# Softmax of chunked attention: exp and row sums by chunk on ScalarE instead of one exp between VectorE steps

## The chip, the cores and the metric

The kernel runs on one core of a Trainium2 chip. The metric is the device time of one execution in microseconds, the median of several runs. A core has five engines with a queue each: TensorE (matrix products, PE in the profile), VectorE (DVE), ScalarE (ACT), GpSimd (POOL) and SyncE (SP), which here only issues transfers. Each queue is worked off in order. TensorE's clock has two levels, 1.2 and 2.4 GHz; the profile shows the granted level as a share of the upper one.

## The reference

Attention within chunks of 64 positions (8 batches, 8 heads, 576 positions, head size 64), then two feed-forward layers over the 4608 tokens (512 wide, hidden 2048). The softmax adds 1e-9 to its row sums.

```python
scores = scale * np.matmul(q_c, k_c.transpose(0, 1, 2, 4, 3))
scores = scores - np.max(scores, axis=-1, keepdims=True)
attn = np.exp(scores)
attn = attn / (np.sum(attn, axis=-1, keepdims=True) + 1e-09)
out = np.matmul(attn, v_c)
# first layer:  h = x @ w_in;  g = s * relu(h)**2 + b;  y = g @ w_out
# second layer: h = y @ w_in;  g = h * sigmoid(1.702 * h);  out = g @ w_out
```

## The kernel before

The tokens are cut into 9 blocks of 512. For each block, attention works on four pairs of heads: a pair fills 128 partitions (two heads of 64) and 8 chunks of 64 keys, so a tile of scores is 128x512. Every product of the feed-forward layers is done as three products of split numbers (a high part that ScalarE makes by a copy, a low part that VectorE makes by a subtraction). The weights of the first layer arrive as raw words and are decoded by steps that alternate between VectorE, GpSimd and ScalarE before they can be used (`decode`, lines 118 to 133; the split follows in 148 and 149).

The first hidden products (`gemm_in`, line 507, tile h) have two PSUM banks to write to; ScalarE's relu (line 533 for the first two blocks, 519 after) empties one, then it is squared, split (lines 98 and 99) and used two steps later by `gemm_out` (line 577, tiles acc). Blocks 0 and 1 are done first, while weights are still being decoded; then attention of block j+1 runs beside the first layer of block j. From about 870 us on there is no attention any more, only the second layer, in a scheme with fewer products (lines 607 to 796), with the sums of weights that it needs made beforehand (lines 210 to 224).

The softmax stands in `Pair.steps`, lines 300 to 330. Scores are computed on TensorE into a bank (tile sc, line 307). VectorE takes the maximum of each row and chunk (line 315) and subtracts it (line 316), ScalarE takes the exp of the whole tile in one instruction with the scale in it (line 320), VectorE sums each chunk (line 322), adds 1e-9, takes the reciprocal and multiplies (lines 323 to 325). Then p is turned: by 8 transposes on VectorE (line 281) for the later blocks, and by TensorE and a copy (lines 361 and 365) for the early ones. The second product follows (tile xT, lines 291 or 378), and the result is split into xh and xl.

`EarlyPair` is the form for blocks 0 and 1: there, q and k are turned by TensorE (line 348) and copied out of PSUM by ScalarE (lines 353 and 356). The scores and the results xT take turns in two banks (`at_ps`).

The order of the work comes from a list of items with due times (`at`, `steps_at`): each step of a pair, of a weight's decode and of the products has a time in units of half a product group. A planner then simulates the program with its own durations and fixes the order on each queue; a few orders are forced by hand (`behind`, and all transfers that are due before the time 2 * NS, in the order of the list).

Of the kernel before, what the change touches and what calls it, by code (L numbers as in the profile page):

```python
# [10 lines left out]
AF = mybir.ActivationFunctionType  # L11
ALU = mybir.AluOpType
AX = mybir.AxisListType
# [3 lines left out]
P = 128  # L17
CH = 64
# [26 lines left out]
def chunk_attention_two_ffn(ctx, tc, q, k, v, w1_in, w1_out, s, b, w2_in, w2_out, out):  # L45
# [6 lines left out]
    nc = tc.nc  # L52
# [9 lines left out]
    scale = 1.0 / float(D) ** 0.5  # L62
# [33 lines left out]
    def split(hi, lo, src):  # L96

        nc.scalar.activation(out=hi, in_=src, func=AF.Copy)  # L98
        nc.vector.tensor_tensor(out=lo, in0=src, in1=hi.bitcast(F32), op=ALU.subtract)  # L99


    def tmp(name, dtype=F32):
        return tpool.tile([P, NB_MAX], dtype, tag="tmp", name=name)
# [135 lines left out]
    class Pair:  # L239


        def __init__(self, j, hp):
            self.j, self.hp = j, hp
            self.n = sizes[j]
            self.nch = self.n // CH
# [23 lines left out]
        def stage_qk(self):  # L269
            self.qt, self.kt = tmp("qt")[:, 0:self.n], tmp("kt")[:, 0:self.n]  # L270
            for t, src in ((self.qt, self.raw[0]), (self.kt, self.raw[1])):
                nc.vector.transpose(out=t.rearrange("p (u l) -> p u l", l=BK), in_=src)
            yield
            yield
# [21 lines left out]
        def split_x(self, ps):  # L296
            X[0, self.j, self.hp] = xh, xl = new_x()
            split(xh, xl, ps)

        def steps(self):  # L300

            yield from self.stage_qk()
            yield
            ps = at_ps.tile([P, self.nch, CH], F32, tag="at", name="sc")
            for c in range(self.nch):
                for r in heads:
                    nc.tensor.matmul(  # L307
                        out=ps[r, c, :], lhsT=self.qt[r, c * CH:(c + 1) * CH], rhs=self.kt[r, c * CH:(c + 1) * CH],
                        start=True, stop=True,
                    )  # L310
            yield
            mx = spool.tile([P, self.nch], F32, tag="mx", name="mx")
            sm = spool.tile([P, self.nch], F32, tag="sm", name="sm")
            p = tmp("p")[:, 0:self.n].rearrange("p (c t) -> p c t", t=CH)
            nc.vector.tensor_reduce(out=mx, in_=ps, axis=AX.X, op=ALU.max)
            nc.vector.tensor_tensor(
                out=p, in0=ps, in1=mx.unsqueeze(2).to_broadcast([P, self.nch, CH]), op=ALU.subtract
            )
            yield
            nc.scalar.activation(out=p, in_=p, func=AF.Exp, scale=scale)  # L320
            yield
            nc.vector.tensor_reduce(out=sm, in_=p, axis=AX.X, op=ALU.add)
            nc.vector.tensor_scalar(out=sm, in0=sm, scalar1=1e-9, scalar2=None, op0=ALU.add)
            nc.vector.reciprocal(out=sm, in_=sm)
            nc.vector.tensor_tensor(  # L325
                out=p, in0=p, in1=sm.unsqueeze(2).to_broadcast([P, self.nch, CH]), op=ALU.mult
            )
            yield
            turned = self.turn(p)
            yield  # L330
            ps = self.second(turned)
            yield
            self.split_x(ps)
            done[0, self.j] = done.get((0, self.j), 0) + 1

    class EarlyPair(Pair):


        def __init__(self, early, hp):
            super().__init__(early.j, hp)  # L340
# [2 lines left out]
        def stage_qk(self):  # L343
            ps = []
            for x in ("q", "k"):
                ps.append(acc_ps.tile([P, self.n], F32, tag=f"acc{2 * (self.hp % 2) + len(ps)}", name="qkT"))
                for i in range(self.n // P):
                    nc.tensor.transpose(
                        ps[-1][:, i * P:(i + 1) * P], self.early.raw[x, i][:, self.hp * P:(self.hp + 1) * P], ident
                    )  # L350
            yield
            self.qt = tmp("qt")[:, 0:self.n]
            nc.scalar.copy(out=self.qt, in_=ps[0])
            yield
            self.kt = tmp("kt")[:, 0:self.n]
            nc.scalar.copy(out=self.kt, in_=ps[1])
# [489 lines left out]
    def plan_first_weights():  # L846
        for n, (kind, i) in enumerate(order):
            st = {}
            if n < KF:
                t = FIRST - (7 - 2 * n if n < 2 else 2.5 - 1.5 * (n - 2))  # L850
                t_load = FIRST - 20 + 1.5 * n if n < STAGED else t - 5
            else:
                t = FIRST + (15 + 1.5 * i if i < KF // 2 else 24 + 3.5 * (i - KF // 2))
                t_load = t - 5

            def load(kind=kind, i=i, st=st):
                st["st"] = load_first(kind, i)

            def steps(kind=kind, i=i, st=st, n=n):

                old = len(nc.cur_bb.bb.instructions)
                for step, _ in enumerate(first_steps(kind, i, st["st"])):
                    if step == 0:
                        behind(old, DVE, ("lo", n - 2))
                        behind(old, ACT, ("relu", n - 4))
                    yield
                marks["lo", n] = latest(DVE)
            at(t_load, load)
            steps_at([(t + d, 1) for d in (0, 0.8, 1.6, 2.3)], steps, after_x=n >= EARLY)
# [71 lines left out]
```

## Time and profile before

| | |
|---|---|
| time, median of 3 runs | 1655.84 us (1654.95 to 1659.75) |
| the profiled execution | 1655.53 us |
| its span, first to last instruction | 1653.8 us |
| TensorE busy | 1601.2 us, 97% |
| VectorE busy | 1046.3 us, 63% |
| ScalarE busy | 786.0 us, 48% |
| GpSimd busy | 278.8 us, 17% |

The shares of busy time are means over stages with different limits. Products are pipelined, so their durations overlap. In a row of a group, the first number after the bar is its busy time in us, then the mean of one instruction in ns, then the idle time of its engine just ahead of it and what ended it. An instruction that starts before the one ahead of it has ended overlaps with it.

### The profile page before, as it was taken

To read this page: it belongs to the slowest core of one execution; us is meant where nothing else is said; L and a number is where in the kernel's file an instruction comes from. 1 tells how busy PE (TensorE), PEld (TensorE's weight loads), DVE (VectorE), ACT (ScalarE), POOL (GpSimd) and SP (SyncE) were. 2 spreads that over 40 slices of the span, in tenths; PEclk is the share of its full clock that TensorE was granted. 3 is DMA by queue.
4 is the path that set the end of the run, shared out by engine and by line. 5 is a ranking of instruction groups with operands and counts; after the bars stand their busy time and mean duration, and the time that the engine had idled before them with its cause. 6 is when DMAs were issued, how large, how long until landed. Compare 5 with 4: busy or idle time off the path is not lost.

```text
span 1653.8 us, 24616 instructions
## 1 busy us (share of the span) xinstructions
PE 1601.2 (97%) x8936; PEld 1311.6 (79%) x8936; DVE 1046.3 (63%) x1724; ACT 786.0 (48%) x1339; POOL 278.8 (17%) x310
## 2 busy tenths in 40 slices
PE   6879999999999999999999999999999999999998
PEld 4668877778888888888888888878887888788876
DVE  5887765745565565656635443579558946984685
ACT  3766533444544444454446532456345535553552
POOL 1344201223314223232322000010001000100000
PEclk8889999999999999999999999999999999999999
DMA  9435455656555555655456441676868686777764
GB/s 228 116 102 156 122 134 129 149 134 164 132 147 142 138 140 147 159 140 139 127 158 200 139 123 43 192 249 214 205 194 264 183 223 205 254 187 219 217 194 76
DMA packets 398345, 272.19 MB, mean 165 GB/s; under 512 B 255376, under 2 KB 345488, under 8 KB 398224
## 3 DMA queue, kind: packets, MB, share of 16 engines
q1 hardware_dynamic: 390800, 249.64, 55.8%
q0 software_dynamic: 5120, 16.78, 3.1%
q10 hardware_dynamic: 2304, 4.20, 0.7%
q8 instruction: 71, 1.16, 0.3%
q14 instruction: 50, 0.41, 0.1%
HBM read 209.72 MB, written 60.82 MB: 164 GB/s over the span
## 4 chain that ended last, share of the span: by engine, by line
PE 90%; DVE 4%; ACT 2%; DMA 1%; POOL 1%; SPq 1%; issue 1%; ACTq 0%; POOLq 0%
PE acc L577 25%; PE h L507 23%; PE x L682 11%; PE x L777 11%; PE d L682 5%; PE d L777 5%; PE b L777 3%; PE b L682 3%; PE sc L307 2%; PE xT L291 2%; POOL wm L130 0%; SPq L255 0%; DVE wi L126 0%; DVE p L325 0%; DVE wi L149 0%
## 5 line engine op out<-in xcount | busy, mean ns | idle before, releaser
L507 PE MATMUL h<-xh,wi 128*128 128x512 f32 x1280 | 402.0, 396 | 17.6 <-ACT r L519 6.1
L577 PE MATMUL acc<-gh,wo 128*128 128x512 f32 x1152 | 356.7, 393 | 2.3 <-ACT gh L98 2.3
L507 PEld LDWEIGHTS h<-xh,wi 128*128 128x128 f32 x1280 | 240.0, 190 | 70.7 <-ACT r L519 7.9
L577 PEld LDWEIGHTS acc<-gh,wo 128*128 128x128 f32 x1152 | 215.3, 189 | 48.4 <-ACT gh L98 2.5
L507 PE MATMUL h<-xl,wi 128*128 128x512 f32 x640 | 250.6, 393 | 0.0
L577 PE MATMUL acc<-gl,wo 128*128 128x512 f32 x576 | 223.1, 392 | 0.0
L99 DVE TENSOR_TENSOR gl<-r,gh 128x512 fp32r<-128x512 f32 x128 | 95.4, 746 | 144.6 <-ACT gh L98 144.2
L507 PEld LDWEIGHTS h<-xl,wi 128*128 128x128 f32 x640 | 121.5, 190 | 26.0
L519 ACT ACTIVATE r<-h 128x512 f32<-128x512 f32 x112 | 66.3, 592 | 147.5 <-PE h L507 141.6
L577 PEld LDWEIGHTS acc<-gl,wo 128*128 128x128 f32 x576 | 108.4, 189 | 23.4 <-DVE gl L99 0.6
L130 POOL TENSOR_TENSOR wm<-wm,wc 128x512 int32<-128x512 int32 x52 | 72.2, 1392 | 293.5 <-DVE wm L126 129.6
L754 ACT ACTIVATE op<-wo 128x512 fp32r<-128x512 f32 x128 | 79.5, 630 | 79.3 <-PE d L777 25.8
L704 DVE TENSOR_TENSOR wo<-wo,r 128x512 f32<-128x512 f32 x96 | 66.0, 691 | 63.0 <-ACT r L703 62.6
L777 PE MATMUL x<-op,wi 128*128 128x512 f32 x432 | 104.4, 389 | 0.0
L621 POOL DMA_DIRECT2D xr<-y x32 | 17.2, 539 | 507.1 <-ACT r L703 262.8
L682 PE MATMUL x<-xh,wi 128*128 128x512 f32 x320 | 99.6, 391 | 3.1 <-DVE wo L701 3.1
L281 DVE STREAM_TRANSPOSE pt<-p 32x256 f32<-32x256 f32 x224 | 97.7, 436 | 3.9
L703 ACT ACTIVATE r<-wo 128x512 f32<-128x512 f32 x96 | 60.8, 633 | 76.7 <-DVE wo L701 76.0
L777 PEld LDWEIGHTS x<-op,wi 128*128 128x128 f32 x432 | 81.1, 188 | 16.9
L755 DVE TENSOR_TENSOR op<-wo,op 128x512 fp32r<-128x512 f32 x128 | 85.2, 680 | 7.4 <-ACT op L754 6.0
L218 ACT ACTIVATE wst<-wst 128x896 fp32r<-128x896 f32 x32 | 30.5, 953 | 119.2 <-POOL wst L216 69.1
L98 ACT ACTIVATE gh<-r 128x512 fp32r<-128x512 f32 x128 | 80.5, 629 | 13.5 <-DVE r L523 11.0
(148 smaller groups left out, 2768.2 us busy)
## 6 DMA issues: line engine op xcount, KB each, us to landing
wi<-wo_sums SPq DMA_DIRECT2D x112, 512.0 KB, 4.3
wi<-wi_sums SPq DMA_DIRECT2D x96, 512.0 KB, 3.7
wst<-in_moe_w_out SPq DMA_DIRECT2D x32, 512.0 KB, 4.5
wi_sums<-wst SPq DMA_DIRECT2D x32, 448.0 KB, 3.6
wo_sums<-wst SPq DMA_DIRECT2D x32, 448.0 KB, 3.5
wst<-in_moe_w_in SPq DMA_DIRECT2D x24, 512.0 KB, 5.1
y<-ost SPq DMA_DIRECT2D x36, 256.0 KB, 3.7
xr<-y POOLq DMA_DIRECT2D x32, 256.0 KB, 6.2
```

The lines of the kernel that those rows point to most:

```text
L98: nc.scalar.activation(out=hi, in_=src, func=AF.Copy)
L99: nc.vector.tensor_tensor(out=lo, in0=src, in1=hi.bitcast(F32), op=ALU.subtract)
L130: nc.gpsimd.tensor_tensor(out=t, in0=t, in1=c.bitcast(I32), op=ALU.add)
L281: nc.vector.transpose(out=pt[r.start + ek * BK:r.start + (ek + 1) * BK, :, eq * BK:(eq + 1) * BK], in_=p[r.start + eq * BK:r.start + (eq + ...
L507: nc.tensor.matmul(out=ps, lhsT=w_[:, kk, :], rhs=x_, start=kk == 0 and a == 0, stop=kk == KD - 1 and a == 2,)
L519: nc.scalar.activation(out=r, in_=ps, func=AF.Relu)
L577: nc.tensor.matmul(out=acc[m], lhsT=l_, rhs=r_, start=i == 0 and a == 0, stop=i == KF - 1 and a == 2)
L682: nc.tensor.matmul(out=self.ps[key], lhsT=l_, rhs=r_, start=start and k == 0 and a == 0, stop=k == HK - 1 and a == 2, skip_group_check=not ...
L704: nc.vector.tensor_tensor(out=g, in0=h, in1=r, op=ALU.mult)
L754: nc.scalar.activation(out=hi, in_=src, func=AF.Copy)
L755: nc.vector.tensor_tensor(out=lo, in0=src, in1=hi.bitcast(F32), op=ALU.subtract)
L777: nc.tensor.matmul(out=self.ps[key], lhsT=l_, rhs=r_, start=start and i == 0 and a == 0, stop=i == HF - 1 and a == 2, skip_group_check=not ...
```

## The change

After the maximum, VectorE no longer subtracts. The maximum is negated and scaled in its small tile, and eight instructions on ScalarE, one for each chunk of 64 columns, read the scores from PSUM, multiply by the scale, add the negated maximum as a bias from that tile, take the exp and give the row's sum as a second output. VectorE's sum over the tile is gone. In the early blocks the copy of q multiplies by -scale, so the scores come out negated and scaled, their minimum is the bias as it is, and the exp takes them times -1.

```diff
+        def bias(self, mx, ps):
+
+            nc.vector.tensor_reduce(out=mx, in_=ps, axis=AX.X, op=ALU.max)
+            nc.vector.tensor_scalar(out=mx, in0=mx, scalar1=-scale, scalar2=None, op0=ALU.mult)
+            return scale
+
...
-            nc.vector.tensor_reduce(out=mx, in_=ps, axis=AX.X, op=ALU.max)
-            nc.vector.tensor_tensor(
-                out=p, in0=ps, in1=mx.unsqueeze(2).to_broadcast([P, self.nch, CH]), op=ALU.subtract
-            )
-            yield
-            nc.scalar.activation(out=p, in_=p, func=AF.Exp, scale=scale)
-            yield
-            nc.vector.tensor_reduce(out=sm, in_=p, axis=AX.X, op=ALU.add)
+            to_exp = self.bias(mx, ps)
+            yield
+            for c in range(self.nch):
+                nc.scalar.activation(
+                    out=p[:, c, :], in_=ps[:, c, :], func=AF.Exp, scale=to_exp, bias=mx[:, c:c + 1],
+                    accum_out=sm[:, c:c + 1],
+                )
+            yield
...
     class EarlyPair(Pair):
 
+        def bias(self, mx, ps):
+
+            nc.vector.tensor_reduce(out=mx, in_=ps, axis=AX.X, op=ALU.min)
+            return -1.0
...
-            nc.scalar.copy(out=self.qt, in_=ps[0])
+            nc.scalar.activation(out=self.qt, in_=ps[0], func=AF.Copy, scale=-scale)
```

## Rows read from the trace of the kernel before

**Rows 1.** The page: busy us, share and count; the granted clock in 40 slices.

```profile
PE 1601.2 (97%) x8936; PEld 1311.6 (79%) x8936; DVE 1046.3 (63%) x1724; ACT 786.0 (48%) x1339; POOL 278.8 (17%) x310
...
PEclk8889999999999999999999999999999999999999
```

**Rows 2.** Stretches: length, then busy us of PE, PEld, DVE, ACT, POOL; clock; DMA.

```profile
0.00:45.00 45.00, 27.94 (x326) 20.82 (x327) 25.92 (x51) 17.71 (x33) 4.54 (x9) 0.87 1.08 226
45.00:125.00 80.00, 67.05 (x498) 52.65 (x497) 66.25 (x106) 55.09 (x103) 30.58 (x22) 0.88 0.35 105
...
260.00:350.00 90.00, 83.53 (x574) 66.99 (x573) 52.64 (x92) 35.61 (x59) 24.30 (x28) 1.00 0.58 145
350.00:860.00 510.00, 510.00 (x3326) 420.98 (x3325) 289.52 (x520) 236.73 (x391) 156.99 (x182) 1.00 0.54 140
```

**Rows 3.** One line's instructions, the exp: ns min/median/max, first and last start.

```profile
L320 ACT ACTIVATE p<-p x36: 615/630/635, 14.0 to 811.9; 128x512 f32<-128x512 f32 x36
```

**Rows 4.** TensorE's waits, 0 to 130 us: total, times, longest.

```profile
PE h L507 <- ACT r L533: 5.8, 4, 2.8
...
PE h L507 <- DVE wi L149: 3.8, 1, 3.8
```

**Rows 5.** The chain of waits, first pair: start us, us, what.

```profile
13.32 0.70 DVE p L316
...
15.43 0.18 DVE sm L323
```

**Rows 6.** Groups by line and shape, ScalarE.

```profile
L592 ACT ACTIVATE ost<-acc,shift,sb 128x512 f32<-128x512 f32 x18 | 13.8, 770 | 2.0 <-PE acc L577 1.7
...
L98 ACT ACTIVATE xh<-xT 128x256 fp32r<-128x256 f32 x16 | 5.5, 382 | 5.9 <-PE xT L378 5.8
...
L596 ACT COPY ost<-acc 128x512 f32<-128x512 f32 x2 | 1.2, 588 | 6.0 <-PE acc L577 6.0
L188 ACT COPY shift<-bw 128x4 f32<-128x4 f32 x1 | 0.2, 162 | 1.7 <-PE bw L185 1.7
```

**Rows 7.** The chain of waits, early stretch: start us, us, what.

```profile
61.31 0.60 DVE p L316
...
106.99 0.70 DVE sm L322
...
112.94 5.70 PE acc L577 x12
...
136.12 2.72 PE acc L577 x12
```

**Rows 8.** ScalarE in order of time, 0 to 45 us: start, us, instruction [idle before].

```profile
10.41 0.59 ACT L353 COPY qt<-qkT 128x512 f32<-128x512 f32 x1
10.89 0.60 ACT L356 COPY kt<-qkT 128x512 f32<-128x512 f32 x1
...
24.61 0.69 ACT L122 ACTIVATE wi<-wo 128x512 int32<-128x512 uint32 x1 [1.19 <-DMA wo<-in_moe_w_in]
```

**Rows 9.** ScalarE in order of time, from 43 us: two of its gaps.

```profile
67.11 0.67 ACT L122 ACTIVATE wi<-wst 128x512 int32<-128x512 uint32 x1 [1.96 <-DVE wi L126]
...
90.64 0.67 ACT L131 ACTIVATE wc<-wst 128x512 f32<-128x512 f32 x1 [1.37 <-POOL wm L130]
```

**Rows 10.** The chain of waits, 255 to 350 us.

```profile
268.48 0.70 DVE mx L315
...
295.37 3.02 PE h L507 x12
```

**Rows 11.** A full stretch in order of time: ScalarE, VectorE, then TensorE.

```profile
414.80 0.58 ACT L519 ACTIVATE r<-h 128x512 f32<-128x512 f32 x1
...
412.01 3.60 DVE L281 STREAM_TRANSPOSE pt<-p 32x256 f32<-32x256 f32 x8
...
419.04 0.61 PE L507 MATMUL h<-xh,wi 128*128 128x512 f32 x2
...
421.85 1.15 PE L291 MATMUL xT<-pt,vs 64*64 64x64 f32 x32
```

## The prediction

> **What bounds the kernel now.** I read the page first: busy times and granted clock. TensorE is busy 1601.2 of 1653.8 us, VectorE 63%, ScalarE 48% [rows 1]. So only the 52.6 us in which TensorE stands still, and what the clock takes in the first slices, can move at all. Then the table of stretches: of those 52.6 us, 45.00 - 27.94 = 17.1 lie before 45 us, 80.00 - 67.05 = 13.0 from 45 to 125, 90.00 - 83.53 = 6.5 from 260 to 350, and none from 350 to 860 [rows 2]. The remaining 16 us or so come after 860, where there is no softmax any more: its 36 exps run from 14.0 to 811.9 us [rows 3]. The change therefore works on two places with idle TensorE time and on one long stretch without any. Third, the waits of TensorE in the first 130 us: the first hidden product waits 3.8 us for decoded weights, and later products wait 5.8 us for their bank, which ScalarE's relu has not emptied [rows 4]. In that part the bound is the two engines that decode the weights, VectorE (66.25 of 80 us busy) and ScalarE (55.09 of 80), with TensorE at an average clock of 0.88, so partly at 1.2 GHz [rows 2].
>
> **The change, part by part.** Per pair of heads (36 of them, 8 early ones before 125 us, 28 later) VectorE loses the subtraction and the sum over 128x512. Each costs 0.70 us in a free chain and 0.60 us in a packed queue [rows 5, 7], so 1.2 to 1.4 us per pair. The 28 later pairs gain one scaling of 128x8, whose like took 0.18 us [rows 5]; the early ones have it in their copy of q, which stays one instruction on ScalarE and which I cost at nothing: it already reads the bank and writes the same tile.
>
> ScalarE loses one exp of 0.63 us [rows 3] and gains eight of 128x64. No row shows an exp of that size or one with a second output. From a copy out of PSUM of 512 columns (588 ns) and one of 256 (382 ns) a column is 0.80 ns, so 64 columns take 382 - 192 x 0.80 = 228 ns. Scale and bias read from tiles made the 128x512 line take 770 instead of 588 ns, so one such operand is 91 ns [rows 6]. That is 0.32 us each; two copies back to back start 0.48 us apart though they take 0.59, an overlap of 0.11 [rows 8]. Lower bound 0.21 us a piece, if the sum comes out for nothing; upper bound 0.32 + 0.16 = 0.48, if reading out the sum is one more instruction as long as the 128x4 copy [rows 6] and nothing overlaps. I take the middle, 0.34: a burst of 2.7 us (1.7 to 3.8). ScalarE's queue thus gets 2.7 - 0.52 = 2.2 us longer per pair. In the free chain of the first pair, from the start of the subtraction (13.32) to the add that follows the sum (15.43), 2.1 us pass now [rows 5]; then 2.7, plus 0.2 in later pairs. So the softmax of one pair gets about 0.6 us later (early) or 0.8 us later (later pairs). VectorE waits for the exp already now, at the sum; it will wait at the add, and behind that stand decode steps and the low halves of products: this is in the sums below. The scores' bank is held some 2 us longer, at no cost, since the pair's second product takes the other bank of the two. No transfer is moved, and nothing on SyncE's or GpSimd's queue.
>
> On the price of the burst, the Trainium skill, ScalarE: Activation LUTs, section What ACT_TABLE_LOAD costs, speaks against the change: an activation has a fixed part of about 280 ns when its bias is a pointer, 0.833 ns per column on top, and neighbours overlap by some 93 ns. By that (an estimate from the page) eight pieces take 8 x 0.24 + 0.09 = 2.0 us, without the readout of the sums, on which it gives no price; the burst would be 0.7 us shorter than mine and the sum below 4 x 0.7 = 2.8 us lower. The trace agrees on the parts it shows (overlap 0.11 us, operand 91 ns, slope 0.80).
>
> *Before 45 us*, four early pairs: -0.7 us. The subtractions and sums leave VectorE while it begins to decode. But ScalarE waits 1.19 us at 24.61 for the weights themselves [rows 8], so the first hidden product can come only about one VectorE instruction earlier. If the burst is 3.8 us, each pair is 1.7 us later instead, and its weights' decode behind it: bounds -2.0 and +1.7.
>
> *45 to 125 us*, the other four early pairs: +2.0 us. The chain of waits holds seven of their eight subtractions and sums (0.60 to 0.70, together 4.4 us; first and last in [rows 7]). They go. Four bursts come, 4 x 2.2 = 8.8 us more on ScalarE, and queued behind each are decode steps of weights, which VectorE waits for, and relus, for whose banks TensorE waits. ScalarE's queue has gaps after the first and third of these pairs, 1.96 us at 67.11 and 1.37 at 90.64 [rows 9], so I let a quarter of each burst vanish: 6.6 - 4.4 = 2.2, rounded to 2.0 since the last pair's mend the wait it already has. Bounds: -4.4 (bursts all in gaps) and +8.8 (VectorE's relief worth nothing).
>
> *260 to 350 us*: +0.8 us. Here a later pair's softmax is in the chain: max at 268.48, then through the turned p, an output, the decode of the second weights and transfers to the product at 295.37 [rows 10]. That path gets 0.8 us longer. ScalarE's own path (outputs and relu right behind the exp) gets 2.7 + 0.2 - 0.72 - 0.52 = 1.7 us longer, but waits that follow take up the difference. Bounds 0 and +1.7.
>
> *125 to 260 and 350 to 860 us*: 0. TensorE is full, and what covers the bursts is the distance between relu and the use of its bank. In the tight case shown, the relu at 414.80 ends at 415.38 and the group of products that needs a free bank starts at 419.04: 3.7 us for a burst that adds 2.2. The turned p is there at 415.61 and used at 421.85: 6.2 us for 0.8 [rows 11]. If that cover were gone each pair would cost up to 2.2 us, 62 us for 28; I allow two such pairs, +4, in the range.
>
> Sum: -0.7 + 2.0 + 0.8 + 0 = +2.1 us. The profiled execution took 1655.53 us (span 1653.8), 0.3 under the median of 1655.84, so 1658 us as a median. What a measurement of this kernel can tell from no change is about 0.3%, 5 us: the forecast is "no difference".
>
> **Rivals.** (1) *VectorE was the bound*: the bursts fall into ScalarE's gaps, and the 4.4 us of chain and another 1 to 2 before 45 us are gained: -0.7 - 4.4 = -5.1, at best -6.4, so 1650 us. For it: VectorE is the busier one of the two from 45 to 125 us, 83% against 69% [rows 2], and the chain holds its instructions, not the exps. Against: ScalarE would then be at (55.09 + 8.8)/80 = 80%, no freer than VectorE is now. (2) *ScalarE's queue becomes the wait*, between 45 and 113 us: each burst of the second block's four pairs stands ahead of a decode step and a relu, and nothing of VectorE's relief is used: +8.8, with +1.7 at 268 and about 0.5 before 45, 1667 us. It decides once a piece costs 0.40 us or more, or when bursts meet relus for whose bank TensorE already waits 5.8 us [rows 4]; against it stand the gaps of [rows 9]. (3) *Another order*: each queue's order comes from a planner that simulates the program with its own durations, and 252 more ScalarE instructions and other lengths give it another plan, also far from the softmax. A wait for a bank reached 2.8 us here [rows 4], and after a gap the 12 products at 112.94 took 5.70 us, where 12 of the same line at 136.12 took 2.72 (3.0 us lost, at the lower of the clock's two levels, 1.2 GHz for 2.4) [rows 7]; one of each and a little more is +8, 1664 us. (4) *The sums are not had for less*: if reading one out takes longer than the 128x4 copy, the work has only moved to ScalarE and grown; that is rival 2 with a burst over 3.8 us, and its chance is in there.
>
> **How the numbers follow.** Forecast 0.50 (its own range 1651 to 1661), rival 1 0.20, rival 2 0.20, rival 3 0.10. Faster by over 0.3% is rival 1: 0.20. Slower by over 0.3% is rivals 2 and 3: 0.30. Within: 0.50. The range reaches from rival 1's best (1649) to rival 2 (1667); beyond lie perhaps 2 in 10, the mishaps in full stretches above all.
>
> **What would show it.** In the changed profile: L316 and the 128x512 sum gone, VectorE some 45 us less busy; eight exps of 128x64 about 0.32 us long, starting 0.34 apart; ScalarE about 75 us busier; TensorE's busy time as before and 350 to 860 us still full; the idle time from 45 to 125 us at about 15 instead of 13.0. Rival 1 shows as a first full stretch that begins 5 us earlier, rival 2 as more waiting for relu or for decoded weights right after each early burst, rival 3 as waits far from any burst. The prediction is wrong if TensorE has new idle time after 350 us, or if the idle time before 125 us moves by more than 5 us either way.

## The result, and the profile after

The changed kernel takes 1668.03 us (median of 4 runs, 1666.82 to 1669.23) against 1656.16 for the kernel before on the same chip: ratio 1.0067, 95% interval 1.0051 to 1.0083, some 12 us slower. The forecast was 1658.0 and "no difference"; the time lies 1 us above the upper end of its range.

First the page of after, with its span and the busy time of each engine, as in [rows 1]:

```profile
span 1665.8 us, 25132 instructions
...
PE 1600.2 (96%) x8936; PEld 1310.7 (79%) x8936; DVE 1009.8 (61%) x1680; ACT 850.2 (51%) x1879; POOL 280.1 (17%) x310
```

TensorE does the same work as before (1600.2 us for 1601.2). The 12 us are time in which it stands still. VectorE has 36.5 us less to do and ScalarE 64.2 more. The groups of ScalarE show that each exp of 64 columns is two instructions, the exp itself and the readout of its sum, which overlap:

```profile
L324 ACT ACTIVATE p<-sc,mx 128x64 f32<-128x64 f32 x288 | 86.3, 326 | 49.0 <-DVE mx L303 26.6 <-DVE mx L346 13.5 <-issue 6.8
...
L324 ACT ACTIVATION_READ_ACCUMULATOR p<-sc,mx 128x1 f32 x288 | 63.2, 219 | 0.0
```

The stretches of after, with the columns of [rows 2] and one more stretch, 125 to 260:

```profile
0.00:45.00 45.00, 25.66 (x300) 19.42 (x304) 19.63 (x38) 22.29 (x88) 5.08 (x9) 0.96 1.01 222
45.00:125.00 80.00, 59.58 (x507) 46.19 (x504) 59.70 (x96) 60.34 (x159) 26.93 (x19) 0.91 0.34 100
125.00:260.00 135.00, 134.74 (x775) 109.34 (x774) 91.65 (x147) 72.16 (x175) 37.76 (x26) 1.00 0.51 138
260.00:350.00 90.00, 85.08 (x576) 68.62 (x575) 48.82 (x90) 41.67 (x117) 20.58 (x24) 0.98 0.55 133
350.00:860.00 510.00, 505.62 (x3322) 416.25 (x3321) 268.11 (x494) 269.13 (x683) 153.74 (x180) 1.00 0.53 138
```

TensorE's idle time from 45 to 125 us is now 80.00 - 59.58 = 20.4 us (13.0 before), before 45 us it is 19.3 (17.1), and 350 to 860 us, full before, has 4.4. Since stretches of equal time don't hold equal work, I also use the *lag*: the start of the n-th product of 512 columns in one kernel less its start in before. In after it is +2.0 us at 45 us, +0.5 at 61, where the second block's first burst starts, +5.7 at 125, +6.2 at 330, +9.4 at 350, +11.9 at 860 and +12.1 at the end. So half of the loss falls before 125 us, where eight pairs are worked off, and half near the later 28.

What TensorE waits for in the first 130 us of after (in us: total, times, longest; before it was [rows 4]):

```profile
PE h L517 <- ACT r L543: 12.6, 5, 4.7
...
PE sc L313 <- ACT kt L366: 4.7, 2, 4.3
...
PE qkT L358 <- DVE xl L99: 3.0, 1, 3.0
```

Waits for relu have grown from 5.8 to 12.6 us. ScalarE's timeline shows why. Lines of readouts and of most exps are left out; the bracket is the idle time ahead of an instruction:

```profile
13.42 0.31 ACT L324 ACTIVATE p<-sc,mx 128x64 f32<-128x64 f32 x1 [2.79 <-DVE mx L346]
...
15.75 0.64 ACT L363 ACTIVATE qt<-qkT 128x512 f32<-128x512 f32 x1
16.22 0.63 ACT L366 COPY kt<-qkT 128x512 f32<-128x512 f32 x1
...
75.53 0.64 ACT L98 ACTIVATE xh<-xT 128x256 fp32r<-128x256 f32 x2
78.40 0.31 ACT L324 ACTIVATE p<-sc,mx 128x64 f32<-128x64 f32 x1 [2.23 <-DVE mx L346]
...
80.63 0.24 ACT L324 ACTIVATION_READ_ACCUMULATOR p<-sc,mx 128x1 f32 x1
80.72 0.64 ACT L543 ACTIVATE r<-h 128x512 f32<-128x512 f32 x1
```

And TensorE's timeline beside it:

```profile
16.91 1.33 PE L313 MATMUL sc<-kt,qt 64*64 64x64 f32 x20 [4.26 <-ACT kt L366]
...
72.57 0.69 PE L388 MATMUL xT<-pt,wo 64*64 64x64 f32 x32
73.09 1.11 PE L313 MATMUL sc<-kt,qt 64*64 64x64 f32 x32
74.13 0.65 PE L358 MATMUL qkT<-ident,wo 128*128 128x128 f32 x4
77.82 0.66 PE L358 MATMUL qkT<-ident,wo 128*128 128x128 f32 x4 [3.03 <-DVE xl L99]
81.41 1.22 PE L517 MATMUL h<-xh,wi 128*128 128x512 f32 x2 [2.93 <-ACT r L543]
```

A burst lasts from 13.42 to 15.75, 2.33 us. The second pair's copies of q and k stand behind the first burst, at 15.75 and 16.22; in before they ran at 10.41 and 10.89, ahead of the exp [rows 8]. By 72.6 us both banks of the hidden products were full, so the rows show nothing that the relu at 80.72 waited for but its place in the queue. ScalarE stood still for 2.2 us, waiting for the maximum, then did the burst, then the relu. TensorE did two groups of transposes (qkT) in that time and waited 3.03 and 2.93 us. In before, hidden products stood between these two groups:

```profile
72.27 1.11 PE L348 MATMUL qkT<-ident,wo 128*128 128x128 f32 x4
73.03 1.20 PE L507 MATMUL h<-xh,wi 128*128 128x512 f32 x2
...
76.52 0.60 PE L348 MATMUL qkT<-ident,wo 128*128 128x128 f32 x4
```

The clock adds to the gap. TensorE was busy for 0.66 of the 4.4 us from 74.8 to 79.2, and from 79.2 to 86.0 us the granted clock was 0.50, which is 1.2 of 2.4 GHz: the twelve hidden products from 81.41 on took 5.2 us, the twelve from 86.75 on 3.0. Before has such a stretch too, but half as long (71.0 to 74.4).

The later half, on ScalarE around 345 us and on TensorE:

```profile
344.73 0.95 ACT L218 ACTIVATE wst<-wst 128x896 fp32r<-128x896 f32 x1 [9.66 <-POOL wst L216]
345.58 0.58 ACT L529 ACTIVATE r<-h 128x512 f32<-128x512 f32 x1
```

```profile
346.21 0.73 PE L517 MATMUL h<-xh,wi 128*128 128x512 f32 x2 [1.79 <-ACT r L529]
...
355.61 1.20 PE L517 MATMUL h<-xh,wi 128*128 128x512 f32 x2 [2.57 <-ACT r L529]
...
427.88 0.50 PE L587 MATMUL acc<-gl,wo 128*128 128x512 f32 x1 [1.49 <-DVE gl L99]
```

There a relu stands behind a step of the weight sums, which waits for GpSimd; the burst before it had ended ten us earlier, at 334.9. But the same stands in before:

```profile
338.25 0.95 ACT L218 ACTIVATE wst<-wst 128x896 fp32r<-128x896 f32 x1 [10.77 <-POOL wst L216]
339.11 0.58 ACT L519 ACTIVATE r<-h 128x512 f32<-128x512 f32 x1
```

From 125 to 860 us TensorE waits 7.5 us for relus in after and 6.1 in before, so these rows alone don't explain the later half. Two small things come on top: 2.1 us of waits for VectorE that before doesn't have, and a clock of 0.96 from 260 to 300 and 0.89 from 345 to 360 us, where before has 1.00.

### The profile page after: what moved, and what is told of

Its sections match the earlier page's. It is cut to its first block, busy times and chain, and to the rows that moved or that the text cites. A ratio compares the mean times of both kernels' runs of the same rounds, so it can differ in the third digit from the quotient of the medians.

```text
span 1665.8 us, 25132 instructions
## 1 busy us (share of the span) xinstructions
PE 1600.2 (96%) x8936; PEld 1310.7 (79%) x8936; DVE 1009.8 (61%) x1680; ACT 850.2 (51%) x1879; POOL 280.1 (17%) x310
## 4 chain that ended last, share of the span: by engine, by line
PE 83%; DVE 5%; SPq 3%; ACT 3%; DMA 3%; POOL 1%; issue 1%; ACTq 0%; POOLq 0%; DVEq 0%
PE h L517 22%; PE acc L587 21%; PE x L692 11%; PE x L787 11%; PE d L692 5%; PE d L787 5%; PE b L692 3%; PE b L787 3%; SPq L255 2%; PE sc L313 2%; PE xT L291 1%; ACT p L324 1%; POOL wm L130 1%; SPq L265 1%; DVE wi L149 1%
## 5 line engine op out<-in xcount | busy, mean ns | idle before, releaser
L517 PE MATMUL h<-xh,wi 128*128 128x512 f32 x1280 | 404.3, 398 | 25.4 <-ACT r L543 12.6
L99 DVE TENSOR_TENSOR gl<-r,gh 128x512 fp32r<-128x512 f32 x128 | 102.2, 799 | 138.8 <-ACT gh L98 138.2
L324 ACT ACTIVATE p<-sc,mx 128x64 f32<-128x64 f32 x288 | 86.3, 326 | 49.0 <-DVE mx L303 26.6
```

The source lines that it names most:

```text
L324: nc.scalar.activation(out=p[:, c, :], in_=ps[:, c, :], func=AF.Exp, scale=to_exp, bias=mx[:, c:c + 1], accum_out=sm[:, c:c + 1],)
L517: nc.tensor.matmul(out=ps, lhsT=w_[:, kk, :], rhs=x_, start=kk == 0 and a == 0, stop=kk == KD - 1 and a == 2,)
```

## The experiments

Each time is a median of 5 to 11 runs, and each ratio is to before on the same chip (1656.6 to 1656.8 us there), with its 95% interval. The theories: **the burst** (rival 2: ScalarE's queue is longer, so everything behind it is later), **the order** (rival 3: the planner puts the queues in another order), and one that came from the traces, **the claim**. Tile p is one of the shared pool `tmp` of ten buffers, from which relu's tiles (r), the turned q and k and decode's tiles come too. On a queue, the first writers of these tiles stand in the order in which the program asks for them. The traces bear that out for ScalarE up to 130 us: the copies of q and k and the relus come in one and the same order in before, after and all other kernels. In before p's first writer is VectorE's subtraction. In after it is the first exp, so a relu whose tile is asked for after p must stand behind that exp on ScalarE, even while the exp waits for the maximum.

### Which pairs

```diff
-            to_exp = self.bias(mx, ps)
+            if isinstance(self, EarlyPair):   # later_only: if not isinstance(...)
+                ...                           # the new softmax
+            else:
+                ...                           # the old one (later_only: q copied without a factor)
```

**early_only.** 

> The new softmax in the eight early pairs alone; the 28 later pairs keep subtraction, one exp and sum. In the trace of after, the products are 5.7 us late from 125 us on, and another 6.3 us come after 330 us. Bursts (rival 2): the 5.7 us come back here and nothing else, about 1661.8 us. Order of the planner alone (rival 3): no sum, any time from 1652 to 1668, and new waits far from any burst. VectorE's relief worth something in the later pairs: then this kernel must be slower than after minus 6.3, and the time would lie above 1662.

**later_only.** 

> The new softmax in the 28 later pairs alone; the eight early ones as before. Bursts: the idle time before 125 us is that of before (17 and 13 us), TensorE's waits at about 345, 427 and 674 us come back with 6.3 us, about 1662.5 us. If those waits hang on where the early part left the transfers and weight sums (the product stream 5.7 us late meets the sums of weights elsewhere), they don't come back: 1656 to 1658. Order of the planner alone: anything from 1652 to 1668.

Measured: early_only 1664.65, 1.0048 (1.0034 to 1.0062); later_only 1661.27, 1.0026 (1.0018 to 1.0035). The two losses, 0.48% and 0.26%, together make 0.74%, the 0.67% of after within their intervals: the halves are separate, and each comes without the other. The early pairs cost 3 us more alone than expected. In early_only the same waits stand as in after (12.6 us for relu, 4.3 for kt), and the lag is +6.2 at 125 us.

### The claim taken away

```diff
-            p = tmp("p")[:, 0:self.n].rearrange("p (c t) -> p c t", t=CH)
+            p = self.qt.rearrange("p (c t) -> p c t", t=CH)
```

**new_p_in_q.** 

> After, but p lives in the tile of qt, which is dead once the scores are made, and claims no buffer of the shared pool. The bursts have the same length and place of need. Theory of the claimed buffer: in after the first writer of p is an exp, so every relu, copy or decode step on ScalarE whose tile is handed out later than p's has to stand behind the burst, which waits for the maximum; with that gone ScalarE can take ready relus ahead of the burst, and most of the 12 us go: 1656 to 1660. Theory of the burst's length (rival 2): the queue is as long as in after, 1666 to 1669. Order alone: another number without a reason, 1654 to 1668.

**old_p_in_q.** 

> Before, with p in the tile of qt: the control for the kernel with the new softmax and p there. Claimed buffer: p's first writer is VectorE's subtraction, nothing on ScalarE waits for the claim, so 1655 to 1657. If the tenth buffer that comes free is worth something by itself, this kernel gains as well, 1650 to 1654. Order alone: up to 5 us either way.

Measured: new_p_in_q 1654.54, 0.9989 (0.9980 to 0.9998); old_p_in_q 1652.15, 0.9974 (0.9963 to 0.9984). With bursts as they were, the loss is gone; the time lies below the 1656 to 1660 that the claim foretold, as the buffer that comes free has a worth of its own. A buffer more is worth 4 us to the old kernel, and between these two kernels the change costs 0.15%, 2.4 us, where with p in the pool it costs 12.

To tell the claim from the buffer that comes free, VectorE touches p first, and, the other way round, the old exp claims it:

```diff
             p = tmp("p")[:, 0:self.n].rearrange("p (c t) -> p c t", t=CH)
+            nc.vector.memset(p[:, 0, 0:1], 0.0)        # new_touch: after
             to_exp = self.bias(mx, ps)
...
-                out=p, in0=ps, in1=mx.unsqueeze(2).to_broadcast([P, self.nch, CH]), op=ALU.subtract
+                out=d, in0=ps, in1=mx.unsqueeze(2).to_broadcast([P, self.nch, CH]), op=ALU.subtract
-            nc.scalar.activation(out=p, in_=p, func=AF.Exp, scale=scale)
+            nc.scalar.activation(out=p, in_=d, func=AF.Exp, scale=scale)   # old_exp_claims; d is qt's tile
```

**new_touch.** 

> After, with one tiny instruction more per pair: VectorE sets one column of p to zero ahead of the maximum (the exp overwrites it). Bursts, sizes and number of buffers are as in after, but the first writer of p's buffer is VectorE again, as in before. Theory of the claimed buffer: 36 instructions of about 0.1 us are paid on VectorE and most of the 12 us go, 1656 to 1661. If instead the gain of the kernel with p in the tile of qt came from the buffer that is left free, this stays at 1666 to 1669. Burst: 1666 to 1669.

**old_exp_claims.** 

> Before, with one edit: the subtraction writes into the dead tile of qt, and the one exp reads that and writes p. The instructions, their sizes and their number are those of before; only the first writer of p's buffer in the shared pool is now an exp on ScalarE, as in after. Theory of the claimed buffer: relus, copies and decode steps whose tiles are handed out after p's must stand behind the exp on ScalarE, so most of the loss comes without any burst: 1661 to 1668. Theory of the burst: nothing is longer, 1655 to 1657. Order alone: up to 5 us either way.

Measured: new_touch 1658.43, 1.0013 (1.0004 to 1.0022); old_exp_claims 1654.29, 0.9988 (0.9979 to 0.9997). The first went as the claim has it: 36 more instructions on VectorE and the kernel is 9.6 us faster than after. ScalarE, in new_touch:

```profile
68.67 1.10 ACT L544 ACTIVATE r<-h 128x512 f32<-128x512 f32 x2
...
73.72 0.31 ACT L325 ACTIVATE p<-sc,mx 128x64 f32<-128x64 f32 x1 [0.73 <-DVE mx L347]
```

The relus stand ahead of the burst, and the burst comes at 73.72 instead of 78.40. But the second refutes the claim by itself: there the relus do stand behind the exp, and it costs nothing. TensorE's waits for relus aren't a price by themselves either: before 130 us they are 9.2 us here, between the 5.8 of before and the 12.6 of after. ScalarE, in old_exp_claims:

```profile
70.82 0.61 ACT L321 ACTIVATE p<-qt 128x512 f32<-128x512 f32 x1
71.34 0.58 ACT L534 ACTIVATE r<-h 128x512 f32<-128x512 f32 x1
```

So neither a burst without the claim nor a claim without the burst makes the loss.

### Instructions and order exchanged

Every queue can be held to the order of another kernel (with p in qt's tile, so that no claim stands against it). The exps stand where the one exp stood; the subtraction goes right behind the maximum, the sum right ahead of the add:

```diff
+    for one, two in zip(row, row[1:]):      # row: all instructions, in the other kernel's order
+        tc.add_manual_dep(two, one.name, IN_ORDER, reason="fixed order")
```

**old_in_new_order.** 

> The old softmax (subtraction, one exp, sum; p in the tile of qt) with every queue held to the order of after: the exp stands where the burst's last exp stood, the subtraction right behind the maximum, the sum right ahead of the add. Order alone (rival 3): the order carries the loss, 1664 to 1668. Burst alone (rival 2 as it was forecast): without bursts nothing is lost, 1655 to 1658. Both together (the order puts relus and copies behind the exp, but only a burst of 2.3 us makes that dear): one exp of 0.6 us in that place costs little, 1657 to 1661.

**new_in_old_order.** 

> The new softmax (bursts with row sums; p in the tile of qt) with every queue held to the order of before: the eight exps stand where the one exp stood, the scaling where the subtraction stood. Relus that stood ahead of the exp still do. Order alone: 1655 to 1658. Burst alone: 1664 to 1668. Both together: the burst costs what was forecast for it, about 2 us, 1657 to 1660.

Measured: old_in_new_order 1664.84, 1.0046 (1.0033 to 1.0059); new_in_old_order 1657.86, 1.0010 (1.0001 to 1.0019). The order of after, with not one burst in it, carries 8 of the 12 us. The bursts, in the order of before, cost 1 to 2. TensorE in old_in_new_order has the two groups of transposes side by side as in after, and the waits around them:

```profile
68.87 1.22 PE L507 MATMUL h<-xh,wi 128*128 128x512 f32 x2 [2.61 <-ACT r L533]
...
74.84 0.66 PE L348 MATMUL qkT<-ident,wo 128*128 128x128 f32 x4
77.05 0.66 PE L348 MATMUL qkT<-ident,wo 128*128 128x128 f32 x4 [1.56 <-DVE xl L99]
79.58 1.22 PE L507 MATMUL h<-xh,wi 128*128 128x512 f32 x2 [1.87 <-ACT r L533]
```

I had thought that the claim hurts because each burst holds up a relu as it runs. That would have left old_in_new_order at 1657 to 1661, and it fell. Most of the loss is made when the order is planned. No kernel was held to its own order as a control; that holding is cheap is seen from new_in_old_order.

The same exchange between the two kernels with p in qt's tile:

**new_in_old_q_order.** 

> The new softmax, p in the tile of qt, with every queue held to the order of the old softmax with p there (1652.2). Burst priced by itself, as between before and the new softmax in its order (1.3 us): 1653 to 1656. If the burst's price was hidden there by chance: 1657 to 1661.

**old_in_new_q_order.** 

> The old softmax, p in the tile of qt, with every queue held to the order of the new softmax with p there (1654.5). If that order is a good one and the burst costs 1 to 2 us: 1652 to 1655. If the order holds a loss that the burst's relief on VectorE pays back: 1656 or more.

Measured: 1658.38, 1.0006 (0.9998 to 1.0015), and 1655.69, 0.9991 (0.9983 to 1.0000). By the ratios, the bursts cost 0.32% (5 us) in the order planned for the old softmax, and nothing (0.9989 with them, 0.9991 without) in the order planned for the new one. The first expectation was missed in its main range, and the second time lies between its two ranges. A burst's price isn't one number: it costs nothing that can be told in an order planned with it, and 1.7 and 5 us in two orders planned without it.

### Chance, or a plan that comes of itself?

Small edits that leave the softmax alone or nearly so:

```diff
+            nc.vector.tensor_scalar(out=sm, in0=mx, scalar1=-scale, scalar2=None, op0=ALU.mult)  # tiny_more: before; new_tiny: after
...
-            nc.scalar.activation(out=self.qt, in_=ps[0], func=AF.Copy, scale=-scale)   # new_plain_early: after,
+            nc.scalar.copy(out=self.qt, in_=ps[0])                                     # and no EarlyPair.bias
```

**tiny_more.** 

> Before, with one tiny instruction of 128x8 more on VectorE per pair, behind the maximum, whose result is overwritten: how far the planner's order and the time move without a cause of weight. Order alone (rival 3): several us, 1651 to 1664. Other theories: 36 times 0.06 us on VectorE, at most 0.5 us of it before 125 us, so 1656 to 1657.

**new_tiny.** 

> After, with one tiny instruction of 128x8 more on VectorE per pair behind the maximum, whose result is overwritten. Claim and burst are as in after; the planner gets another number of instructions. If the claim with the burst makes the slow order: 1664 to 1670. If the order is chance: anywhere from 1652 to 1668, most likely about 1658.

**new_plain_early.** 

> After, but the early pairs form their bias as the later ones do (maximum, then one scaling of 128x8 on VectorE, 0.1 to 0.2 us in the chain of each), and q is copied without a factor. Claim and burst as in after. If the claim with the burst makes the slow order: 1664 to 1671. If the order is chance: 1652 to 1668, most likely about 1658.

Measured: tiny_more 1656.84, 1.0000 (0.9991 to 1.0009); new_tiny 1670.86, 1.0071 (1.0057 to 1.0085); new_plain_early 1668.40, 1.0071 (1.0059 to 1.0084). Chance falls: one more instruction moves nothing in before, and three kernels with claim and burst, whose orders differ in places, have about the same loss.

### How long a burst

```diff
                     out=p[:, c, :], in_=ps[:, c, :], func=AF.Exp, scale=to_exp, bias=mx[:, c:c + 1],
-                    accum_out=sm[:, c:c + 1],
                 )
...
+            nc.vector.tensor_reduce(out=sm, in_=p, axis=AX.X, op=ALU.add)      # no_readout: both
...
-            for c in range(self.nch):                                         # no_readout_long: this as well
+            for c in [*range(self.nch), 0, 1, 2]:
...
+            nc.vector.tensor_reduce(out=sm, in_=p, axis=AX.X, op=ALU.add)      # readout_and_sum: after, and this alone
```

**no_readout.** 

> Eight exps by chunk with bias, but no second output: VectorE sums the tile as before. p in its own tile of the shared pool, claimed by the first exp. The burst has eight pieces some 0.2 us apart in place of 0.29, 1.6 to 1.9 us, and VectorE keeps a sum of 0.6 us per pair. Claim and burst together: the relus still stand behind a burst, 0.5 to 0.7 us shorter, 1662 to 1668. If reading out the sums is what costs: 1656 to 1659. Order alone: any of these.

**no_readout_long.** 

> The kernel without second outputs (1654.7), with three of its eight exps issued a second time, which write the same values again: the burst is 11 pieces of 0.21 us, about 2.4 us, as long as that of after; VectorE keeps its sum; p is claimed by the first exp. If the claim with a burst of over 2 us makes the slow order: 1663 to 1670. If it is the second output, or VectorE's missing sum: 1655 to 1659.

**readout_and_sum.** 

> After, with VectorE's sum over the tile kept beside the second outputs (it writes the same sums over them): 36 times 0.60 to 0.70 us more on VectorE. If the claim with the long burst makes the slow order: 1666 to 1673. If it is VectorE's missing sum, which lets the planner put other work there: 1655 to 1660.

Measured: no_readout 1654.69, 0.9988 (0.9979 to 0.9997); no_readout_long 1664.39, 1.0045 (1.0033 to 1.0058); readout_and_sum 1669.40, 1.0082 (1.0068 to 1.0096). ScalarE, in no_readout, then in no_readout_long:

```profile
72.33 1.71 ACT L324 ACTIVATE p<-sc,mx 128x64 f32<-128x64 f32 x8
73.90 0.63 ACT L543 ACTIVATE r<-h 128x512 f32<-128x512 f32 x1
```

```profile
78.42 1.71 ACT L324 ACTIVATE p<-sc,mx 128x64 f32<-128x64 f32 x8
79.99 0.63 ACT L543 ACTIVATE r<-h 128x512 f32<-128x512 f32 x1
80.47 0.77 ACT L324 ACTIVATE p<-sc,mx 128x64 f32<-128x64 f32 x3
```

Eight exps without readout take 1.57 us to the next instruction (72.33 to 73.90), 0.20 a piece, and with that the claim costs nothing: the expectation of 1662 or more was missed. Three more exps per pair, which compute nothing new, cost 9.7 us, and this pair's softmax comes 6 us later, as in after. Neither the readout as such nor VectorE's missing sum parts the kernels with the loss from the others. With the claim, exps of 0.6 to 1.6 us per pair are free here, 2.2 to 2.3 us are not. But the length doesn't work by holding up a relu as the burst runs: in the rows of no_readout_long the relu goes ahead of the three extra exps, behind 1.57 us as in no_readout.

What parts the kernels with the loss from those without it in the traces is where the planner put the maximum. Up to that of the last early pair, the copies of q and k, the relus and the first exps stand in the same order on ScalarE in all ten kernels in which the early exps claim p or are held to after's order, with the loss or without it (with it: after, new_tiny, new_plain_early, readout_and_sum, early_only, no_readout_long, old_in_new_order; without it: no_readout, one_exp, old_exp_claims). VectorE's order is not the same. Here it is in after, then in no_readout: the copy of the turned p, the decode step of line 133, and the maximum that the next burst waits for:

```profile
70.03 0.68 DVE L375 COPY pt<-pT 128x512 f32<-128x512 f32 x1
...
74.27 0.69 DVE L133 SCALAR_TENSOR_TENSOR wi<-wi 128x512 f32<-128x512 f32 x1 [0.20 <-ACT wi L131]
...
77.68 0.68 DVE L346 TENSOR_REDUCE mx<-sc 128x8 f32<-128x512 f32 x1
```

```profile
67.74 0.68 DVE L375 COPY pt<-pT 128x512 f32<-128x512 f32 x1
...
71.43 0.68 DVE L346 TENSOR_REDUCE mx<-sc 128x8 f32<-128x512 f32 x1
72.45 1.07 DVE L133 SCALAR_TENSOR_TENSOR wi<-wi 128x512 f32<-128x512 f32 x1 [0.34 <-ACT wi L131]
```

In all seven kernels with the loss, steps of line 133 stand ahead of this maximum, which starts 5.7 to 7.7 us after the copy; in the three others they stand behind it, and it starts 3.6 to 3.9 us after the copy. So the claim puts a relu behind the exp, and the plan with the longer burst puts the exp's maximum behind a weight's decode. The kernel old_p_in_q has a late maximum too (7.3 us) but its relus ahead of the exp, and loses nothing. That the two together make the early loss fits all these traces; no run moved the maximum alone.

### A version that beats both

One maximum per row over all chunks, scaled to a bias of one column; one exp of 128x512 from PSUM; VectorE's sum kept. The softmax is the same but for the 1e-9, which now stands beside sums scaled to the row's maximum instead of the chunk's: a chunk whose scaled scores all lie some 20 below that maximum would be changed by it, as exp(-20) is 2e-9.

```diff
-            nc.vector.tensor_reduce(out=mx, in_=ps, axis=AX.X, op=ALU.max)
-            nc.vector.tensor_tensor(
-                out=p, in0=ps, in1=mx.unsqueeze(2).to_broadcast([P, self.nch, CH]), op=ALU.subtract
-            )
+            top = mx[:, 0:1]
+            nc.vector.tensor_reduce(out=top, in_=ps, axis=AX.XY, op=ALU.max)
+            nc.vector.tensor_scalar(out=top, in0=top, scalar1=-scale, scalar2=None, op0=ALU.mult)
             yield
-            nc.scalar.activation(out=p, in_=p, func=AF.Exp, scale=scale)
+            nc.scalar.activation(out=p, in_=ps, func=AF.Exp, scale=scale, bias=top)
```

**one_exp_p_in_q.** 

> A candidate without bursts: one maximum per row over all eight chunks (the softmax does not change by it), scaled to a bias of one column, one exp of 128x512 straight from PSUM with that bias, and VectorE's sum as before; p in the tile of qt. VectorE loses the subtraction (0.6 to 0.7 us) for a scaling (0.1 to 0.2), ScalarE's exp stays one instruction. Theory of the claimed buffer with VectorE's relief worth something before 125 us: 1648 to 1652, below the kernel before with p in the tile of qt (1652.2). If VectorE's relief is worth nothing: 1652 to 1654. Order alone: up to 5 us either way.

**one_exp.** 

> One maximum per row over all chunks, scaled to a bias, one exp of 128x512 straight from PSUM, VectorE's sum; p in its own tile of the shared pool, whose first writer is then the exp on ScalarE. Against the same kernel with p in the tile of qt (1647.0): if a claim on ScalarE is cheap as long as the exp is short, 1647 to 1651; if the claim by itself costs, 1655 to 1659.

Measured: one_exp_p_in_q 1646.98, 0.9947 (0.9934 to 0.9959); one_exp 1649.18, 0.9953 (0.9941 to 0.9966), so the claim of one exp of 0.7 us costs nothing that can be told. The time of one_exp_p_in_q lies 1 us below its range. The page and ScalarE's group of one_exp_p_in_q:

```profile
span 1644.1 us, 24631 instructions
...
PE 1594.5 (97%) x8936; PEld 1307.9 (80%) x8936; DVE 1034.2 (63%) x1724; ACT 790.5 (48%) x1339; POOL 279.8 (17%) x310
```

```profile
L319 ACT ACTIVATE qt<-sc,mx 128x512 f32<-128x512 f32 x36 | 24.7, 687 | 61.1 <-DVE mx L317 49.6 <-PE acc L576 3.4 <-issue 3.3
```

VectorE gets only a third of the relief that it has in after (1034.2 us busy, before 1046.3, after 1009.8), but ScalarE keeps its one exp per pair (790.5 us busy, before 786.0). By itself the free buffer is worth 4.4 us (old_p_in_q) and this softmax 7.4 (one_exp); together they give 9.8. The lag is -5.5 us at 125 us and -9.6 at 330.

## Why the prediction was wrong, point by point

*The parts were right or on the safe side.* Pieces start 0.29 us apart (forecast 0.34, bounds 0.21 and 0.48), a burst takes 2.33 us (2.7), VectorE loses 36.5 us (some 45) and ScalarE gains 64.2 (some 75). The readout is one more instruction, and at 219 ns longer than the 162 that rival 4 names, but overlapped it adds only 0.29 - 0.20 = 0.09 us to a piece, so the burst stays below rival 4's 3.8 us. The Trainium skill, ScalarE: Activation LUTs, section What ACT_TABLE_LOAD costs, gave an estimate of 2.0 us for eight pieces without readout, to the end of the last; no_readout has 1.71, so the trace lies below the page too. By it the forecast would have been lower, so it spoke for the change and not, as I wrote, against it; the kernel was slower, with a burst shorter than I took.

*The sum holds for the order it was made in.* It was worked out with every queue in the order of before, and there the bursts cost a ratio of 1.0010 (1.0001 to 1.0019), 1.7 us (forecast 2.1). That the two agree so well is partly luck: in new_in_old_order's trace the lag grows by 2.3 us between 350 and 860 us, where 0 was forecast, and in old_p_in_q's order the same bursts cost 5 us.

*The step that failed* is the term for 45 to 125 us, "I let a quarter of each burst vanish: 6.6 - 4.4 = 2.2": it takes for granted that ScalarE does relus and decode steps in its gaps as before and that only the burst's length comes on top. The lag grows by 3.7 us there instead of 2.0, and by 5.2 from 61 us on. It is +2.0 at 45 us, where -0.7 stood. The second pair's copies of q and k went behind the first burst there, but that isn't shown to be the cause: new_touch, whose copies stand ahead of it, has +2.3 at 45 us, and old_exp_claims, whose copies stand behind the exp, -2.1. The list of what the change moves lacked one thing: the first write to p goes from VectorE's queue to ScalarE's, and the pool's order goes with it; then the planner made another order, in which the next maximum stands behind a weight's decode. The gaps of [rows 9] were no cover, as the same gaps are in after (2.23 us at 78.40) and a ready relu may not use them.

*"350 to 860 us: 0"* failed as well: the lag grows there by 2.5 us, after 3.4 between 260 and 350, where +0.8 stood. later_only shows that the later pairs bring this loss by themselves. Why is not settled: moving the claim back to VectorE left a lag of 4.6 us to come after 125 us in new_touch's trace, a free buffer 2.4 in that of new_p_in_q, and the forced order 3.9 in that of new_in_old_order. One trace can differ from its median by 2 or 3 us, so these can't be told apart. Both signs that the prediction had named for being wrong came: 4.4 us of new idle time from 350 to 860 us, and 9.7 us more of it before 125.

*The rivals.* Rival 2 named the right time, 1667, by a mechanism that the runs refute in its plain form: bursts in the old order cost 1 to 5 us, not 12. Its second condition (bursts that meet relus for whose bank TensorE already waits) is what after's trace shows, and so is its sign, more waiting for relu behind the early bursts; but old_in_new_order has such waits without a burst (1.87 us at 79.58), so the sign doesn't tell rivals 2 and 3 apart. Rival 3 had the mechanism, another order, and it got a chance of 0.10 as an accident of durations. The runs show that it is none: the loss comes in all five kernels in which each pair has over 2 us of exps that claim p (after, new_tiny, new_plain_early, readout_and_sum, no_readout_long), and in none of five without the one or the other (new_p_in_q, new_touch, old_exp_claims, one_exp, no_readout; new_touch alone of them is slower than before, by 0.13%). By what rule the planner turns a longer claim into a worse order stays open: I have its orders, not its reckoning. Rival 1 is out for this change, as even in before's order the bursts gain nothing. The kernel one_exp, 6.5 us ahead of before at 125 us, suggests that VectorE's relief is worth something early on if ScalarE doesn't pay for it; its order is another too, so the share of the relief isn't shown.

## What to carry to other kernels

When a step goes from one engine to another, ask which buffer it is the first to write, and what else on the new engine takes buffers from the same pool: all of that may have to stand behind it, while it waits. Then look at what the step itself waits for: here the claim of the early exps went with a loss only where their maximum came late. A tile that is dead anyway was the better place for both softmaxes here, or no worse (one_exp). If a change moves the time by more than its instructions can explain, exchange instructions and orders between the two kernels: that parts the price of the work from the price of the plan.

## What the runs showed of the hardware

A row sum as the second output of an exp on ScalarE is an instruction of its own in the trace, of 219 ns in the mean; it starts 0.2 us after its exp and the next exp starts 0.09 us after it, so that eight exps with readout take 2.33 us and without 1.57. And the 396 exps of 128x64 of no_readout_long, from PSUM with a bias from a tile, took 344 ns in the mean but started 0.20 us apart: the mean of one overstates a burst by some 70%.
